# Window attention ahead of two gated networks: the mask as four 64x64 fp32 products, and the end of attention written out

## Chip, cores and metric

The kernel runs on one core of a Trainium2 chip. The metric is the device time of one execution in microseconds. Of the engines, PE is TensorE (PEld its weight loads), DVE is VectorE, ACT is ScalarE, POOL is GpSimd, and SP issues the DMAs.

## What is computed

```python
scores = scale * np.matmul(q, k.transpose(0, 1, 3, 2))     # 4 batches, 8 heads, 576 positions, 64 wide
rel = pos[:, None] - pos[None, :]
mask = (rel >= 0) & (rel < 64)
scores = np.where(mask, scores, -1000000000.0)
attn = np.exp(scores - np.max(scores, axis=-1, keepdims=True))
attn = attn / (np.sum(attn, axis=-1, keepdims=True) + 1e-09)
x = np.matmul(attn, v)                                      # then 2304 tokens x 512
g = x @ w_gate; x = (g / (1 + np.exp(-g)) * (x @ w_val)) @ w_out        # 512 -> 1536 -> 512
out = ((x @ w1) * (x @ w2) @ w3) @ w_out2                   # 512 -> 1024 -> 1024 -> 512
```

The weights of the two networks come as 64-bit floats, and are narrowed on the chip.

## The kernel before, in words

Attention comes first. A unit is a pair of heads of one batch, 16 units in all. A query block of 64 positions needs the keys of its own block and of the one before it, 128 in all; three such blocks of a pair make a subtile of 128 rows (64 of each head) by 3 x 128 scores, in one PSUM bank. A step m of the loop takes two subtiles, 2m and 2m + 1; there are NM = 24 steps. The work of a step is spread over four of them, so that engines overlap: `emit_S` (the mask and the scores) and `emit_max` in step m, `emit_exp` of its two subtiles at the end of step m and in step m + 1, `emit_norm` in m + 1 (reciprocal of the sums on VectorE, the products on GpSimd), `emit_PT` (transposes of the probabilities) in m + 2, `evac_PT` (their copies from PSUM to the tile ptt, on VectorE) and `emit_PV` (the products with v) in m + 3, whose result `evac_PV` copies to the tiles X on ScalarE. `emit_T` transposes q and k for coming units, two or three parts a step, and `evac_T` copies them. Each engine runs its instructions in the order in which this loop emits them.

The mask is added by TensorE: for each subtile, one product of a scaled 128x128 identity `identr` with a tile of 128 x 384 mask values opens the accumulation, both of the type that TensorE reads as rounded fp32 (F32R). The scores are then 64x64 products of q with 128 key columns, of plain fp32; `place` puts the two heads of a subtile in quarters of the array such that four products, of two subtiles and two heads, use four different quarters. A product of plain fp32 shows as two records in the trace, one of F32R as one.

Between these instructions a planner (`Plan`) sets work for the first network. It keeps a clock `now`, and for each engine the time until which it is taken (`free`, raised by `charge`); `advance(us)` moves the clock on and emits queued jobs of engines that are free before it. Jobs are the narrowing and splitting of weights (w_g, w_v; st_g and st_v are what is loaded), and the operands of the first network (xo): X is cut in quarter blocks, sums of blocks are formed, and each is cast to F32R on ScalarE (`cast`, L200) with the remainder formed on VectorE (`rest`, L204; sums are L208). An operand is ready once both are done. `slots` counts tiles of 128 x 768 words that are free for jobs; ATTENTION = 26 of 56 are kept for attention until its end.

The first network multiplies by a scheme of seven products in place of eight (numbered 1, 2, 5, 6, 7, 4, 3 in order); each is six F32R instructions of 384 columns. Its products are emitted by the generator `gate`, one for each `next`. In the last three rounds of the loop (m = 24, 25, 26), where there is no S, `during_attention` takes 3, 2 and 2 products from `gate`. xo is made for three blocks of 768 tokens; names such as xo0_51 stand for block 0, product 5, second half.

Of the kernel before, what the change touches and what calls it, by code (L numbers as in the profile page):

```python
# [7 lines left out]
F32 = mybir.dt.float32  # L8
F32R = mybir.dt.float32r
I32 = mybir.dt.int32  # L10
I64 = mybir.dt.int64
AF = mybir.ActivationFunctionType
# [4 lines left out]
P = 128  # L17
# [15 lines left out]
def window_attention_moe_kernel(ctx: ExitStack, tc: tile.TileContext, q, k, v, w_gate, w_val, w_out, w1, w2, w3, w_out2, out):  # L33
    nc = tc.nc
# [5 lines left out]
    KC = DM // P  # L40
# [20 lines left out]
    def slot(shape, dtype, name, counted=True):  # L61

        plan.slots -= counted
        return sl.tile(shape, dtype, tag="s", name=name)
# [266 lines left out]
            X[tp, c] = slot([P, TP], F32, f"X{tp}_{c}")  # L331
        return X[tp, c]

    def attention(events, filling):
        if True:
            ident, identr = own.tile([P, P], F32, name="ident"), own.tile([P, P], F32R, name="identr")
            masktiles = [slot([P, 2, SUB, P], F32R, f"mask{x}", False) for x in range(2)]
            mask = [masktiles[0][:, 0], masktiles[0][:, 1], masktiles[1][:, 0]]

            units = [(b, pr) for b in range(B) for pr in range(PAIRS)]  # L340
# [39 lines left out]
            def evac_T(u, part):  # L380
                which, x = divmod(part, 2)
                o = tbank.pop((u, part)).rearrange("p g n -> p (g n)")
                to = kT if which else qT
                if x == 0:
                    to[u] = slot([P, S], F32, f"{'qk'[which]}T{u}", False)
                dst = to[u][:, S // 2 * x:S // 2 * x + S // 2]
                if which == 0:
                    nc.scalar.mul(out=dst, in_=o, mul=0.125)
                elif x == 1:
                    nc.scalar.copy(out=dst, in_=o)  # L390
                else:
                    nc.vector.tensor_copy(out=dst, in_=o)
# [6 lines left out]
            def emit_S(m):  # L399
                both = (2 * m, 2 * m + 1)  # L400
                for i in both:
                    sc[i] = bank(f"S{i}")[:, :SUB * P].rearrange("p (j k) -> p j k", j=SUB)
                    nc.tensor.matmul(sc[i], lhsT=identr, rhs=mask[i % NSUB], start=True, stop=False)
                for jj in range(SUB):
                    for i in both:
                        u, s = divmod(i, NSUB)
                        j = SUB * s + jj
                        keys = kT[u].rearrange("p (w n) -> p w n", n=64)

                        keys = keys[:, :2] if j == 0 else keys[:, j - 1:j + 1] if j % 2 else keys[:, j - 1:j + 1][:, ::-1]  # L410
                        for h in range(2):
                            r, c = 64 * h, 64 * place(i, h)
                            nc.tensor.matmul(sc[i][c:c + 64, jj, :], lhsT=qT[u][r:r + 64, 64 * j:64 * j + 64],  # L413
                                             rhs=keys[r:r + 64], start=False,
                                             stop=jj == SUB - 1)

            def emit_max(m):
                st = own.tile([P, 4, 2, SUB], F32, tag="stat", name=f"stat{m}", bufs=3)
                for x in range(2):
                    nc.vector.tensor_reduce(out=st[:, 0, x, :], in_=sc[2 * m + x], op=ALU.max, axis=AX.X, negate=True)  # L420
                stat[m] = st
# [91 lines left out]
            for x in ((0, 0), (0, 1), (0, 2), (0, 3), (1, 0)):  # L513
                emit_T(*x)
                evac_T(*x)
            for m in range(NM + 3):

                u0, r = 2 * (m // 3), m % 3
                for u in ((u0 + 3,), (), (u0 + 4,))[r]:
                    if u < U:  # L520
                        load_qk(u)
                for u in ((u0 + 1,), (u0 + 2,), ())[r]:
                    if u < U:
                        load_v(u)
                parts = (((u0 + 1, 1), (u0 + 1, 2), (u0 + 1, 3)), ((u0 + 2, 0), (u0 + 2, 1)),
                         ((u0 + 2, 2), (u0 + 2, 3), (u0 + 3, 0)))[r]
                parts = [x for x in parts if x[0] < U]
                if m < NM:
                    emit_S(m)
                if m >= 3:  # L530
                    evac_PT(m - 3)
                for x in parts:
                    emit_T(*x)
                if m >= 3:
                    emit_PV(m - 3)
                if 2 <= m < NM + 2:
                    emit_PT(m - 2)
                if 1 <= m <= NM:
                    emit_exp(2 * m - 1)
                if m == NM:  # L540

                    nc.scalar.activation(out=masks[:, 0, :1], in_=masks[:, 1, :1], func=AF.Silu)
                if m < NM:
                    emit_max(m)
                for x in parts:
                    evac_T(*x)

                filling(m, NM)
                if 1 <= m <= NM:
                    emit_norm(m - 1)  # L550
                for u in ((), (u0,), (u0 + 1,))[r]:
                    if u < U:
                        pair_v(u)
                if m >= 3:
                    evac_PV(m - 3)
                if m < NM:
                    emit_exp(2 * m)
                events(m, NM)


    PRODUCT = 1.04
# [591 lines left out]

    gate = gated(xop1, left1, order1, AF.Silu, h1d, events1)

    def during_attention(m, NM):
        if m in (1, 3):
            loads(1 + m // 2)
        if m == 3:
            make_to(left1[0, 1], 0)  # L1160
        for tp, first in enumerate((13, 20, NM + 2)):
            if m == first:
                xop1[tp] = Operands([X[tp, c] for c in range(KC)], f"xo{tp}")
        if m < NM:
            plan.fill(("DVE",))
        else:
            for e, cost in (("DVE", (1.6, 1.1, 1.1)), ("ACT", (2.2, 0.5, 0.5)), ("POOL", (1.9, 0.0, 0.0))):
                plan.charge(e, cost[m - NM])
            for _ in range((3, 2, 2)[m - NM]):
                next(gate)  # L1170

    def filling(m, NM):
        if m < NM:
            for e, cost in (("DVE", 2.75), ("ACT", 3.2), ("POOL", 2.6)):
                plan.charge(e, cost)
            plan.advance(3.85, ("ACT", "POOL", "SP"))

    with tc.manual_schedule():
        plan.shut.add("POOL")
        attention(during_attention, filling)  # L1180
        plan.slots += ATTENTION
        plan.ahead = 1.0
        for _ in gate:
            pass
        for _ in project(rows, wos, events_p):
            pass
        on(events2, len(order2) - 6, lambda: make_to(w3s[-1]))
        begin_e, run_e = final(rows2)

        def put_all():  # L1190
            for j in by:
                plan.need(j)
            begin_e()
        on(events2, len(order2) - 4, put_all)
        for _ in gated(xop2, left2, order2, AF.Copy, h2d, events2):
            pass
        run_e()
# [30 lines left out]
```

## Time and profile before

| | |
|---|---|
| median of 3 runs | 848.73 us (847.08 to 850.55) |
| profiled execution | 848.98 us |
| its span, first to last instruction | 847.3 us |
| PE, PEld, DVE, ACT, POOL busy | 97%, 93%, 76%, 53%, 7% of the span |
| mean granted clock of TensorE | 0.996 of full |
| HBM | 160 GB/s over the span |

Busy shares are means over stages with different limits. A line number is that of the kernel before; in the changed kernel lines stand lower (L403 becomes L406, L413 L417, L452 L456, L583 L600). In a timeline, neighbouring instructions of one kind are merged, and what stands in brackets is the idle time of the engine ahead of the row and what ended it.

### The profile page before, as it was taken

The numbers are of one execution on the slowest core, as the hardware profiler recorded it, in microseconds if no ns is written. First come the engines' busy times: TensorE is split into PE (matmuls) and PEld (weight loads), VectorE is DVE, ScalarE is ACT, GpSimd is POOL, SyncE is SP. The second block draws the span as 40 slices with busy tenths as digits, with TensorE's granted clock in tenths as the row PEclk, the third lists the DMA queues.
The fourth block names the chain that finished last, engine by engine and source line by source line (L and its number), as shares of the span: only waits on it lengthen the run. The fifth ranks groups of instructions, "written<-read, shape, count | busy, mean of one in ns | idle before, by whom it ended". The sixth has DMA issues, their size and how long they took to land.

```text
span 847.3 us, 15757 instructions
## 1 busy us (share of the span) xinstructions
PE 822.9 (97%) x5870; PEld 791.6 (93%) x5870; DVE 642.5 (76%) x1364; ACT 451.2 (53%) x1188; POOL 60.8 (7%) x89
## 2 busy tenths in 40 slices
PE   7899878899999999999999999999999999999998
PEld 6688767899999999999999999999999998899998
DVE  4799779878688767976698585778788844788884
ACT  6799855564646464643563362544444423766452
POOL 3467600000000000000000000000000000000000
PEclk9999999999999999999999999999999999999999
DMA  9989200135255324689996851015555329623522
GB/s 203 219 174 211 72 1 38 46 121 189 97 207 191 142 91 162 224 301 385 374 307 183 227 200 50 1 75 161 149 167 170 121 83 353 214 78 124 173 75 75
DMA packets 147516, 136.29 MB, mean 161 GB/s; under 512 B 95088, under 2 KB 114288, under 8 KB 146416
## 3 DMA queue, kind: packets, MB, share of 16 engines
q1 hardware_dynamic: 147440, 135.29, 51.0%
q8 instruction: 46, 0.75, 0.4%
q14 instruction: 30, 0.25, 0.1%
HBM read 92.27 MB, written 42.99 MB: 160 GB/s over the span
## 4 chain that ended last, share of the span: by engine, by line
PE 80%; DMA 7%; DVE 4%; SPq 4%; ACT 4%; issue 1%; ACTq 0%; DVEq 0%
PE ala L583 14%; PE alb L583 13%; PE o L723 12%; PE beb L583 7%; PE bea L583 7%; PE al L947 6%; PE acc L881 5%; PE gaa L583 3%; PE gab L583 3%; PE be L947 3%; DMA wo<-wo 2%; SPq L350 2%; PE PV L466 2%; PE ga L947 2%; ACT pexp L427 1%; PE PT L446 1%
## 5 line engine op out<-in xcount | busy, mean ns | idle before, releaser
L723 PE MATMUL o<-ph,wo 128*128 128x384 f32 x576 | 146.7, 334 | 0.2 <-DVE X L710 0.2
L723 PEld LDWEIGHTS o<-ph,wo 128*128 128x128 f32 x576 | 104.2, 188 | 0.5 <-DVE X L710 0.5
L723 PE MATMUL o<-pl,wo 128*128 128x384 f32 x288 | 96.3, 334 | 0.1
L590 ACT COPY ha<-ala 128x384 f32<-128x384 f32 x90 | 42.7, 478 | 57.6 <-PE ala L583 51.2
L594 DVE TENSOR_TENSOR ha<-ha,bea 128x384 f32<-128x384 f32 x60 | 33.2, 553 | 35.8 <-PE bea L583 19.9
L723 PEld LDWEIGHTS o<-pl,wo 128*128 128x128 f32 x288 | 54.1, 188 | 0.4 <-DVE pl L204 0.4
L427 ACT ACTIVATE pexp<-S,stat 128x128 f32<-128x128 f32 x144 | 53.8, 432 | 0.0
L604 ACT ACTIVATE ha<-ha 128x384 f32<-128x384 f32 x54 | 28.3, 526 | 39.1 <-DVE ha L594 39.1
L204 DVE TENSOR_TENSOR hf<-h,hf 128x384 fp32r<-128x384 f32 x84 | 43.5, 553 | 5.6 <-ACT hf L200 5.6
L200 ACT CAST ph<-pl 128x768 fp32r<-128x768 f32 x36 | 29.2, 836 | 34.4 <-DMA pl<-h 27.7
L200 ACT CAST hf<-h 128x384 fp32r<-128x384 f32 x84 | 39.3, 513 | 13.0 <-DVE h L208 11.4
L204 DVE TENSOR_TENSOR pl<-pl,ph 128x768 fp32r<-128x768 f32 x36 | 33.5, 952 | 13.0 <-ACT ph L200 12.5
L437 POOL TENSOR_TENSOR pexp<-pexp,stat 128x384 f32<-128x384 f32 x48 | 38.7, 826 | 41.7 <-DVE stat L434 37.2
L590 ACT COPY c12b<-alb 128x384 f32<-128x384 f32 x30 | 14.4, 480 | 49.4 <-PE alb L583 49.3
L427 ACT ACTIVATION_READ_ACCUMULATOR pexp<-S,stat 128x1 f32 x144 | 38.3, 270 | 0.0
L594 DVE TENSOR_TENSOR c22b<-c22b,beb 128x384 f32<-128x384 f32 x30 | 16.6, 555 | 27.1 <-ACT c22b L590 27.0
L583 PE MATMUL ala<-xo,w_g_6l 128*128 128x384 f32 x90 | 29.6, 338 | 1.6 <-ACT xo L200 1.0
L420 DVE TENSOR_REDUCE stat<-S 128x3 f32<-128x384 f32 x48 | 24.4, 551 | 7.4 <-PE S L413 7.2
L583 PE MATMUL ala<-xo,w_g_1h 128*128 128x384 f32 x120 | 27.7, 345 | 1.7 <-ACT w_g_1h L200 1.7
L466 PE MATMUL PV<-ptt,v 128*64 128x64 f32 x576 | 22.8, 229 | 5.1 <-DVE ptt L452 2.3
L917 ACT COPY o<-al 128x256 f32<-128x256 f32 x36 | 13.4, 373 | 27.0 <-PE al L947 26.0
L466 PEld LDWEIGHTS PV<-ptt,v 128*64 128x64 f32 x576 | 19.5, 139 | 8.8 <-issue 3.8
(533 smaller groups left out, 2490.2 us busy)
## 6 DMA issues: line engine op xcount, KB each, us to landing
h<-ha SPq DMA_DIRECT2D x60, 384.0 KB, 3.2
pl<-h SPq DMA_DIRECT2D x36, 384.0 KB, 6.4
h<-h SPq DMA_DIRECT2D x24, 384.0 KB, 4.9
st_w<-in_moe_w_dram SPq DMA_DIRECT2D x8, 1024.0 KB, 6.3
st_g<-in_moe_w_gate_dram SPq DMA_DIRECT2D x6, 1024.0 KB, 6.3
st_v<-in_moe_w_val_dram SPq DMA_DIRECT2D x6, 1024.0 KB, 5.5
st_wo<-in_moe_w_out_dram SPq DMA_DIRECT2D x6, 1024.0 KB, 5.4
wo<-by_wo SPq DMA_DIRECT2D x12, 512.0 KB, 3.7
```

Of the source, the lines that this page charges most:

```text
L200: (eng.copy if eng is nc.scalar else eng.tensor_copy)(out=hi(), in_=src())
L204: return plan.job(lambda eng: eng.tensor_tensor(out=lo(), in0=src(), in1=hi().bitcast(F32), op=ALU.subtract), after, slots=slots, DVE=dve( ...
L427: nc.scalar.activation(out=pe[:, jj, :], in_=so[:, jj, :], func=AF.Exp, bias=st[:, 0, x, jj:jj + 1], accum_out=st[:, 1, x, jj:jj + 1])
L437: nc.gpsimd.tensor_tensor(out=pe, in0=pe, in1=st[:, 3, x, :].unsqueeze(2).to_broadcast([P, SUB, P]), op=ALU.mult)
L466: nc.tensor.matmul(pp[64 * h:64 * h + 64, 64 * (SUB * x + jj):64 * (SUB * x + jj) + 64], lhsT=vt[u][e][:, at, h, :], rhs=t[:, x, jj, c:c + ...
L583: nc.tensor.matmul(acc, lhsT=self.wt.ops[p, x][:, m, :], rhs=self.xs.ops[p, m][:, y, :], start=start and n == 0, stop=n == 5, skip_group_c ...
L590: nc.scalar.copy(out=out, in_=src)
L594: nc.vector.tensor_tensor(out=out, in0=x, in1=y, op=ALU.add)
L604: nc.scalar.activation(out=h, in_=src, func=func)
L723: nc.tensor.matmul(acc[m, x], lhsT=wos.tiles[i // 6][:, i % 6, :], rhs=rows[2 * tp + x].words(f, b), start=f == n == 0, stop=f == NF - 1 a ...
L881: nc.tensor.matmul(acc, lhsT=w3T[i][c // 3][:, x, (c % 3) * P:(c % 3) * P + P], rhs=zt[c, y], start=c == k == 0, stop=c == NI - 1 and k == 2)
L947: nc.tensor.matmul(acc, lhsT=self.xs.ops[p, m][:, x, t * P:t * P + P], rhs=right.ops[p, m, y], start=start and n == 0, stop=n == 3 * R - 1 ...
```

## The change

`identr` and the mask tiles become plain fp32. In `emit_S` the two 128x128 products are replaced by four of 64x64, with the rows r of the identity and of the mask and the output rows c that the scores of the same head use.

The loop ends at m = 23, and what was in its last three rounds stands behind it, line by line, with calls of `drain` between: each gives tiles back, charges the engines, and takes a product from `gate` (0, 1, 3), moves the clock (2) or queues the operands of block 2 (4). In step 23 the copies of step 21's transposes stand right behind the maximum, and the planner's filling comes behind the exponentials. The v copies of two units come a step earlier at the end.

`during_attention` gives back some of the 26 kept tiles in steps 18 to 23 (HELD) instead of all at the end. In a step the planner's clock moves by 3.55 instead of 3.85 (3.1 in step 23), with the same charges.

```diff
-            ident, identr = own.tile([P, P], F32, name="ident"), own.tile([P, P], F32R, name="identr")
-            masktiles = [slot([P, 2, SUB, P], F32R, f"mask{x}", False) for x in range(2)]
+            ident, identr = own.tile([P, P], F32, name="ident"), own.tile([P, P], F32, name="identr")
+            masktiles = [slot([P, 2, SUB, P], F32, f"mask{x}", False) for x in range(2)]
...
-                    nc.tensor.matmul(sc[i], lhsT=identr, rhs=mask[i % NSUB], start=True, stop=False)
+                for i in both:
+                    for h in range(2):
+                        r, c = 64 * h, 64 * place(i, h)
+                        nc.tensor.matmul(sc[i][c:c + 64], lhsT=identr[r:r + 64, r:r + 64], rhs=mask[i % NSUB][r:r + 64],
+                                         start=True, stop=False)
...
-            for m in range(NM + 3):
+            for m in range(NM):
...
+                if m == NM - 1:
+
+                    evac_PT(m - 2)
+                else:
+
+                    filling(m)
...
+            emit_PV(NM - 3)
+            emit_exp(2 * NM - 1)
+            emit_norm(NM - 1)
+            evac_PV(NM - 3)
+            nc.scalar.activation(out=masks[:, 0, :1], in_=masks[:, 1, :1], func=AF.Silu)
+            drain(0)
+            for x in range(2):
+                emit_PT(NM - 2 + x)
+                evac_PT(NM - 2 + x)
+                drain(1 + 2 * x)
+                emit_PV(NM - 2 + x)
+                evac_PV(NM - 2 + x)
+                drain(2 + 2 * x)
...
+    HELD = {18: 24, 19: 22, 20: 18, 21: 16, 22: 12, 23: 7}
+    HELD_END = (4, 4, 4, 2, 0)
+    held = [ATTENTION]
+    def hold(n):
+        plan.slots += held[0] - n
+        held[0] = n
+    def operands(tp):
+        xop1[tp] = Operands([X[tp, c] for c in range(KC)], f"xo{tp}")
+    def during_attention(m):
+        if m in HELD:
+            hold(HELD[m])
+        if m in (13, 20):
+            operands(m // 20)
+        plan.fill(("DVE",) if m not in HELD or m < 23 else ("DVE", "ACT"))
+    def filling(m):
+        for e, cost in (("DVE", 2.75), ("ACT", 3.2), ("POOL", 2.6)):
+            plan.charge(e, cost)
+        if m == 23:
+            plan.advance(3.1, ("DVE", "ACT", "POOL", "SP"))
-            plan.advance(3.85, ("ACT", "POOL", "SP"))
+            plan.advance(3.55, ("ACT", "POOL", "SP"))
+    def drain(n):
+        hold(HELD_END[n])
+        for e, cost in (("DVE", (0.4, 1.1, 0.0, 1.1, 0.0)), ("ACT", (3.0, 0.0, 0.6, 0.0, 0.6))):
+            plan.charge(e, cost[n])
+        if n == 4:
+            operands(2)
+        else:
+            next(gate) if n in (0, 1, 3) else plan.advance(0.8)
```

What it moves shows in the order of instructions at three places.

TensorE at the scores of step 20, before and now (S40 and S41 are its subtiles, PT35 transposes of an earlier one, T14 a transpose of keys to come; x2 is two neighbouring instructions):

```order
L446 MATMUL PT35_1778<-ident_128,pexp35_1704 128x128 x3
L403 MATMUL S40_1810<-mask0_130,identr_129 128x384
L403 MATMUL S41_1812<-mask1_131,identr_129 128x384
L413 MATMUL S40_1810<-kT13_1712,qT13_1622 64x128 x2
L413 MATMUL S41_1812<-kT13_1712,qT13_1622 64x128 x2
...
L376 MATMUL T14_2_1829<-ident_128,rawk14_1557 128x96 x3
```

```order
L450 MATMUL PT35_1789<-ident_128,pexp35_1718 128x128 x3
L406 MATMUL S40_1818<-mask0_130,identr_129 64x384 x2
L406 MATMUL S41_1819<-mask1_131,identr_129 64x384 x2
L417 MATMUL S40_1818<-kT13_1726,qT13_1634 64x128 x2
L417 MATMUL S41_1819<-kT13_1726,qT13_1634 64x128 x2
...
L376 MATMUL T14_2_1839<-ident_128,rawk14_1567 128x96 x3
```

Each subtile has two mask products of 64 rows in place of one of 128, two per bank and four in all ahead of the scores; nothing else moves.

VectorE from the maximum of step 23, before (first fence) and now (second):

```order
L420 TENSOR_REDUCE stat23_2084<-S46_2040 128x3
L420 TENSOR_REDUCE stat23_2084<-S47_2042 128x3
L204 TENSOR_TENSOR xo0_51_2038<-X0_1_528,xo0_51_2038 128x384
L208 TENSOR_TENSOR X0_0_447<-X0_2_698,X0_0_447 128x384
L433 TENSOR_SCALAR stat22_2020<-stat22_2020 128x6
L434 RECIPROCAL stat22_2020<-stat22_2020 128x6
L452 COPY ptt21_2103<-PT42_2072 128x384
L452 COPY ptt21_2103<-PT43_2076 128x384
L433 TENSOR_SCALAR stat23_2084<-stat23_2084 128x6
L434 RECIPROCAL stat23_2084<-stat23_2084 128x6
L594 TENSOR_TENSOR ha0_0_0_2137<-ha0_0_0_2137,gaa0_0_2147 128x384
L208 TENSOR_TENSOR X0_1_528<-X0_3_776,X0_1_528 128x384
```

```order
L424 TENSOR_REDUCE stat23_2095<-S46_2049 128x3
...
L456 COPY ptt21_2098<-PT42_2083 128x384
...
L437 TENSOR_SCALAR stat22_2030<-stat22_2030 128x6
...
L437 TENSOR_SCALAR stat23_2095<-stat23_2095 128x6
...
L204 TENSOR_TENSOR xo0_10_2136<-X0_0_455,xo0_10_2136 128x384
L204 TENSOR_TENSOR xo0_11_2139<-X0_1_537,xo0_11_2139 128x384
L204 TENSOR_TENSOR w_v0_2l_2149<-st_v0_461,w_v0_1h_1982 128x256
L208 TENSOR_TENSOR st_v0_461<-st_v0_461 128x2x128
L208 TENSOR_TENSOR X0_0_455<-X0_0_455 128x384
L456 COPY ptt22_2163<-PT44_2155 128x384
...
L204 TENSOR_TENSOR xo0_20_2167<-X0_2_709,xo0_20_2167 128x384
L204 TENSOR_TENSOR xo0_21_2170<-X0_3_789,xo0_21_2170 128x384
```

The copies to ptt21 come ahead of both reciprocals. Behind them stand operands of products 1 and 2 of block 0 and a part of w_val, which before were made in steps 13 to 22; up to the last maximum 27 planned operations stand on VectorE where there were 42 (on ScalarE 13 and 26).

TensorE behind the last scores, before and now (PV products with v, ala, gaa, bea products 1/6/7, 2 and 5 of the first unit, alb product 1 of the next):

```order
L446 MATMUL PT43_2076<-ident_128,pexp43_2016 128x128 x3
L466 MATMUL PV21_2106<-ptt21_2103,v14_0_1730 64x64 x4
...
L446 MATMUL PT45_2123<-ident_128,pexp45_2080 128x128 x3
L583 MATMUL ala0_0_2139<-xo0_10_1297,w_g0_1h_782 128x384 x3
...
L583 MATMUL gaa0_0_2147<-xo0_20_1470,w_g0_1h_782 128x384 x2
...
L583 MATMUL bea0_0_2156<-xo0_50_1974,w_g0_2l_943 128x384 x2
...
L466 MATMUL PV22_2168<-ptt22_2165,v14_1_2029 64x64 x2
...
L446 MATMUL PT47_2185<-ident_128,pexp47_2127 128x128 x3
L583 MATMUL ala0_0_2139<-xo0_60_2191,w_g0_5l_1022 128x384 x2
...
L583 MATMUL alb0_0_2206<-xo0_10_1297,w_v0_1h_1215 128x384 x3
...
L466 MATMUL PV23_2220<-ptt23_2217,v15_0_1896 64x64 x2
...
L583 MATMUL ala0_0_2139<-xo0_70_2234,w_g0_6l_1110 128x384 x2
```

```order
L450 MATMUL PT43_2087<-ident_128,pexp43_2026 128x128 x3
L470 MATMUL PV21_2110<-ptt21_2098,v14_0_1739 64x64 x4
...
L600 MATMUL ala0_0_2135<-xo0_10_2136,w_g0_1h_969 128x384 x3
...
L450 MATMUL PT45_2159<-ident_128,pexp45_2091 128x128 x3
L600 MATMUL gaa0_0_2166<-xo0_20_2167,w_g0_1h_969 128x384 x2
...
L470 MATMUL PV22_2187<-ptt22_2163,v14_1_1974 64x64 x2
...
L450 MATMUL PT47_2208<-ident_128,pexp47_2123 128x128 x3
L600 MATMUL bea0_0_2215<-xo0_50_2216,w_g0_2l_1123 128x384 x3
...
L470 MATMUL PV23_2237<-ptt23_2212,v15_0_1899 64x64 x2
...
L600 MATMUL ala0_0_2135<-xo0_60_2235,w_g0_6h_1306 128x384 x3
...
L600 MATMUL alb0_0_2274<-xo0_10_2136,w_v0_1h_1982 128x384 x3
...
L600 MATMUL ala0_0_2135<-xo0_70_2272,w_g0_6h_1306 128x384 x2
```

PV21 is followed by product 1, then PT44 and PT45, product 2, PV22, PT46 and PT47, product 5 and PV23; before, PT44 and PT45 came first, then products 1, 2 and 5, and two more products stood ahead of PV23.

## Rows read from the trace of the kernel before

**Rows 1.** Windows by stage: PE, PEld, DVE, ACT, POOL busy, PEclk, DMA share, GB/s.

```profile
50.00:65.00 15.00, 15.00 (x271) 12.43 (x269) 14.86 (x39) 14.95 (x73) 9.89 (x15) 1.00 0.81 176
...
95.00:105.00 10.00, 7.82 (x97) 7.02 (x96) 5.60 (x15) 7.41 (x30) 7.37 (x10) 0.83 0.01 2
105.00:115.00 10.00, 6.91 (x75) 5.55 (x73) 6.26 (x13) 3.74 (x10) 0.00 (x0) 1.00 0.00 0
```

**Rows 2.** Timeline of PE in a middle step: start, length, instructions, idle before.

```profile
51.19 0.59 PE L403 MATMUL S<-mask,identr 128*128 128x384 f32 x2
51.71 0.89 PE L413 MATMUL S<-kT,qT 64*64 64x128 f32 x24
52.52 0.72 PE L376 MATMUL T<-ident,rawk 96*128 96x96 f32 x6
...
54.27 0.87 PE L446 MATMUL PT<-ident,pexp 128*128 128x128 f32 x6
54.89 0.59 PE L403 MATMUL S<-mask,identr 128*128 128x384 f32 x2
```

**Rows 3.** Timeline of PE in attention's last steps and behind it.

```profile
91.50 0.60 PE L403 MATMUL S<-mask,identr 128*128 128x384 f32 x2
...
94.59 0.60 PE L403 MATMUL S<-mask,identr 128*128 128x384 f32 x2
...
99.98 1.21 PE L466 MATMUL PV<-ptt,v 128*64 128x64 f32 x24 [2.08 <-issue]
...
102.32 2.06 PE L583 MATMUL ala<-xo,w_g_1h 128*128 128x384 f32 x6
...
107.63 0.94 PE L466 MATMUL PV<-ptt,v 128*64 128x64 f32 x24 [1.17 <-DVE ptt L452]
...
116.62 0.51 PE L583 MATMUL gab<-xo,w_v_1h 128*128 128x384 f32 x2
...
117.66 1.20 PE L583 MATMUL beb<-xo,w_v_5h 128*128 128x384 f32 x6
```

**Rows 4.** Instructions of line L413: engine, operation, nanoseconds of one.

```profile
L413 PE MATMUL S<-kT,qT x576: 269/269/473, 8.5 to 95.7; 64*64 64x128 f32 x192
```

**Rows 5.** Timeline of PE in the first ten steps.

```profile
24.28 0.69 PE L376 MATMUL T<-ident,rawq 96*128 96x96 f32 x6 [2.02 <-DMA rawq<-in_q_dram]
...
27.10 1.05 PE L403 MATMUL S<-mask,identr 128*128 128x384 f32 x2
...
34.45 1.03 PE L466 MATMUL PV<-ptt,v 128*64 128x64 f32 x24 [0.50 <-DVE ptt L452]
...
38.75 0.94 PE L466 MATMUL PV<-ptt,v 128*64 128x64 f32 x24 [0.58 <-ACT pexp L427]
...
44.02 0.59 PE L403 MATMUL S<-mask,identr 128*128 128x384 f32 x2
```

**Rows 6.** DMA queues from 15 to 45 us: packets, MB, share of 16 engines.

```profile
q1 hardware_dynamic: 18222, 6.35, 100.1%
```

**Rows 7.** Waits, 0 to 46 us: total us, times, longest.

```profile
DVE st_v L188 <- DMA st_v<-in_moe_w_val_dram: 1.8, 1, 1.8
```

**Rows 8.** Timeline of DVE behind the last step.

```profile
106.00 1.02 DVE L208 TENSOR_TENSOR X<-X,X 128x384 f32<-128x384 f32 x2
```

**Rows 9.** Timeline of ACT behind the last step.

```profile
97.46 0.37 ACT L427 ACTIVATE pexp<-S,stat 128x128 f32<-128x128 f32 x1
...
98.49 0.52 ACT L200 CAST xo<-X 128x384 fp32r<-128x384 f32 x1
...
100.09 1.28 ACT L542 ACT_TABLE_LOAD   x1
...
109.04 0.94 ACT L200 CAST xo<-X 128x384 fp32r<-128x384 f32 x2
```

**Rows 10.** Waits, 117 to 170 us.

```profile
PE bea L583 <- DVE xo L204: 2.7, 2, 1.7
...
PE ala L583 <- ACT xo L200: 1.6, 2, 1.1
```

More of the change, by code (lines that the diff above doesn't have):

```diff
@@ L332, in x_tile, with attention @@
         return X[tp, c]
-    def attention(events, filling):
+    def attention(events, filling, drain):
         if True:
-            ident, identr = own.tile([P, P], F32, name="ident"), own.tile([P, P], F32R, name="identr")
-            masktiles = [slot([P, 2, SUB, P], F32R, f"mask{x}", False) for x in range(2)]
+            ident, identr = own.tile([P, P], F32, name="ident"), own.tile([P, P], F32, name="identr")
+            masktiles = [slot([P, 2, SUB, P], F32, f"mask{x}", False) for x in range(2)]
             mask = [masktiles[0][:, 0], masktiles[0][:, 1], masktiles[1][:, 0]]
@@ L527, in attention @@
                 parts = [x for x in parts if x[0] < U]
-                if m < NM:
-                    emit_S(m)
+                emit_S(m)
                 if m >= 3:
@@ L535, in attention @@
                     emit_PV(m - 3)
-                if 2 <= m < NM + 2:
+                if m >= 2:
                     emit_PT(m - 2)
-                if 1 <= m <= NM:
+                if m >= 1:
                     emit_exp(2 * m - 1)
[L540 to L544, printed above, removed]
+                emit_max(m)
                 for x in parts:
                     evac_T(*x)
-                filling(m, NM)
-                if 1 <= m <= NM:
+                if m == NM - 1:
+                    evac_PT(m - 2)
+                else:
+                    filling(m)
+                if m >= 1:
                     emit_norm(m - 1)
-                for u in ((), (u0,), (u0 + 1,))[r]:
-                    if u < U:
-                        pair_v(u)
+                for u in (((), (u0,), (u0 + 1,)) if u0 + 2 < U else ((u0,), (u0 + 1,), ()))[r]:
+                    pair_v(u)
                 if m >= 3:
                     evac_PV(m - 3)
-                if m < NM:
-                    emit_exp(2 * m)
-                events(m, NM)
+                emit_exp(2 * m)
+                if m == NM - 1:
+                    filling(m)
+                events(m)
+            emit_PV(NM - 3)
[11 more added lines that the diff above has]
+                drain(2 + 2 * x)
     PRODUCT = 1.04
@@ L1154, in window_attention_moe_kernel @@
     gate = gated(xop1, left1, order1, AF.Silu, h1d, events1)
-    def during_attention(m, NM):
+    HELD = {18: 24, 19: 22, 20: 18, 21: 16, 22: 12, 23: 7}
[9 more added lines that the diff above has]
+            hold(HELD[m])
         if m in (1, 3):
@@ L1160, in during_attention @@
             make_to(left1[0, 1], 0)
[L1161 to L1165, printed above, removed]
-        else:
[L1167 to L1175, printed above, removed]
-            plan.advance(3.85, ("ACT", "POOL", "SP"))
+        if m in (13, 20):
[6 more added lines that the diff above has]
+            plan.advance(3.1, ("DVE", "ACT", "POOL", "SP"))
+        else:
+            plan.advance(3.55, ("ACT", "POOL", "SP"))
[7 more added lines that the diff above has]
+            next(gate) if n in (0, 1, 3) else plan.advance(0.8)
     with tc.manual_schedule():
         plan.shut.add("POOL")
-        attention(during_attention, filling)
-        plan.slots += ATTENTION
+        attention(during_attention, filling, drain)
         plan.ahead = 1.0
```

## Prediction

> **What bounds the kernel now.** I read the stretches first, then TensorE's timeline in one step, then the end of attention, then the waits behind it. In the middle of attention TensorE is busy all of a 15 us stretch, and VectorE and ScalarE nearly so [rows 1]; which of the three sets the pace is told by the timeline: no TensorE instruction there has idle time ahead of it, and one step follows the other after 3.70 us [rows 2]. So TensorE bounds the steps from 9 on; from the mask of step 9 to that of step 22 the pitch is (91.50 - 44.02) / 13 = 3.65 us [rows 3, 5]. VectorE and ScalarE are full because the planner fills them with work for later. The first steps are bound by transfers: the DMA engines are full [rows 6], TensorE waits 2.02 us for q and then runs a while at 1.2 instead of 2.4 GHz (the mask pair takes 1.05 against 0.59) [rows 2, 5]. Behind the last mask (94.59) TensorE works in pieces: 2.08 us idle, product 1 in 2.06 us where six such instructions later take 1.20, another 1.17 us idle for ptt [rows 3]; the granted clock is 0.83 of full from 95 to 105, and VectorE is busy for only 6.26 of the 10 us behind [rows 1]. The first units of the network also wait, for operands [rows 10]. The rest of the run is TensorE at work and the same in both kernels.
>
> **The change part by part.**
>
> *Mask.* In the rows, S is three sets of four 64x64 products with 128 columns each, two records per product. Its 24 records take 0.89 us, of which 0.27 is the length of the last [rows 2, 4]; 0.62 for the five gaps between six sets is 0.12 each, or 0.11 without the weight load that only the first waits for. So a set of four runs at once, and 128 columns cost 0.11 per record, 0.22 per product. The new mask is one set of four with 384 columns, as many columns as all of S: 6 x 0.11 = 0.65 us. The old pair takes 0.52 from its start to that of S (51.19 to 51.71) [rows 2]; six 384-column products of its kind elsewhere give (1.20 - 0.33) / 5 = 0.174 each [rows 3], so 0.35 of it is streaming and 0.17 is the turn from 128 rows to 64. That turn now stands ahead of the mask instead of behind it. Cost: 0.65 - 0.35 = +0.30 us per step. Bounds: +0.13 if no turn is left ahead of the mask (0.65 against 0.52), +0.39 with 0.12 per record (0.74 against 0.35). I take 0.30, since the turn between S and T is also paid [rows 2]. Fourteen steps from 9 to 22 lie wholly on TensorE: 14 x 0.30 = **+4.2 us** at the last mask.
>
> The Trainium skill, "TensorE: Matmul & The Clock Gate", section "Back-to-back issue gap", gives N/2.4 + 2.5 ns per matmul, 56 ns at 128 columns; the rows above show twice that per record, as the 4 passes of true fp32 in "FP8 and Floating Point Precision", section "TensorE Precision Notes", would make it. By the first page alone, with two records, the new mask would cost 0.33 us and the steps would stay as they are, some 849.5 in all; the rows decide for the second.
>
> *First nine steps.* There the 0.30 a step is paid while TensorE would wait anyway. Its 2.02 us wait for q ends when the transfer lands, not earlier or later; four masks, one at the low clock, use up about 1.5 of it, and a wait of 0.5 should not lower the clock as this one did. That spares some 0.5 of the mask pair and as much again in the instructions about it. Two further waits, 0.50 and 0.58 [rows 5], come from VectorE, which stood 1.8 us on a weight transfer in step 6 [rows 7]; in the changed order that instruction comes a step later, behind the landing. Transfers still set the earliest start of steps 5 to 8. Spared 2.0 + 1.0 + 1.1 = 4.1, paid 9 x 0.30 plus 0.3 for the cold first mask = 3.0, and about 0.6 of new waiting for k and q: **-0.5 us** (bounds -1.5 and +2.0).
>
> *Less work between the steps.* The planner now moves on by 3.55 per step instead of 3.85. The order shows what that does: up to the last maximum VectorE gets 27 planned operations instead of 42, ScalarE 13 instead of 26. Given-back tiles do not help: in steps 18 to 22 there are six such operations on VectorE where before there were eleven. While TensorE bounds a step of 3.95 us, that lightening gains nothing. The price is at the end: of block 0's operands nothing is ready, where six casts and rests (xo_10, 11, 20, 21, 30, 50) were, and w_val is split as far as its first product.
>
> *The end*, counted from the last mask. Durations: VectorE on 384 columns 0.47 apiece (two in 1.02) [rows 8]; three exponentials 1.03, a cast 0.41, the table load 1.28 [rows 9]; a product 1.04 (116.62 to 117.66), PV 0.85, PT 0.65 [rows 2, 3]. S ends at 1.6, the maxima at 2.6, ptt of PT 42/43 at 4.2, so PV 21 starts at 4.2, where it started at 5.4: a gain of 1.2. Then product 1 needs xo_10 and xo_11, which ScalarE casts behind exponentials (to 4.7), an eviction and table load (6.9): casts 7.3 and 7.7, rests to 8.2, product 1 ends 8.7, PT 44/45 at 9.5. VectorE has a weight rest, a sum and X_0 to do (9.5), then ptt, xo_20 and xo_21: 11.5; product 2 ends 11.9, PV 22 12.8, PT 46/47 13.5. Then an addition, four weight rests, the last two behind ScalarE's casts (14.1), ptt, xo_50, X_1, a cast and xo_51 to 17.0: product 5 ends 17.4, PV 23 18.3. Two sums and xo_60 follow, and xo_61, cast behind PV's eviction, ends 19.7; product 6 ends 20.1, product 1 of the next unit 21.1; with seven more VectorE operations product 7 ends 23.5. Before it ended at 116.62 - 94.59 = 22.0. So **+1.5 us**, bounds -8.4 (no wait left, second rival) and +6 (third). VectorE's idle time here is what pays most of the late work.
>
> *Behind it.* Two rests of block 0 are still owed (+0.95), two of block 1 are done earlier, and the waits for operands [rows 10] are shortened by as much: **-0.5**, bounds -3 and +1.
>
> Sum: 848.98 (the profiled execution: span 847.3 and 1.7 around it; 0.25 above the median of three) + 4.2 - 0.5 + 1.5 - 0.5 = **853.7 us**.
>
> **The rivals.**
> *The mask costs no more than the pair.* If its two records ran 384 columns as fast as the old kind does, 2 x 0.174 stand against 0.35. For it, sets of four have only been seen with short columns, where four weight loads could be what takes 0.11; against it, the length of one record, 0.269 at 128 columns, against 0.33 for 384 columns of the other type [rows 3, 4], for a third of the columns 0.8 of the length. Then 848.98 - 0.5 + 1.5 - 0.5 = 849.5.
> *Faster: the end wins.* If the operand work keeps ahead of TensorE, nothing waits between the last mask and product 7: S 1.6, four PV, three PT and six products with their turns between make 13.6 where 22.0 stood, -8.4, and part of rows 10 goes too, about -2. Time 848.98 + 3.7 - 10.4 = 842.3. It decides at product 5: xo_51 must be there by about 13.5 on that clock, not 17.0. VectorE's 6.26 of 10 busy [rows 1] speaks for it; the order, with eleven operations between ptt 22 and xo_51, against.
> *The clock falls.* TensorE idles 2.3 us before product 1, as long as where it fell before [rows 3, 5], and again about product 5; five products, PT and PV at half rate add up to 5: 859.
> *The change does not do what it says*: the tiles given back change nothing visible; that is already in the forecast.
>
> **How the numbers follow.** Forecast 0.58, mask for nothing 0.20, end wins 0.12, clock falls 0.10. A measurement here tells 0.5% (4.2 us) from no change: below 844.5 is faster, above 853.0 slower. The forecast's own range, from the bounds of its terms, is 849.5 to 858 and lies above 853.0 in two thirds of cases (0.39); with the last case 0.49 slower. Faster is most of the second rival and a little of the first, 0.14; the rest, 0.37, is the same. The range leaves out the best of the second rival and the worst of the last: 846 to 860.
>
> **What would show it.** Mask records in sets of four, second set 0.33 behind the first, S 0.65 behind the mask; pitch of the middle steps 3.95 with no TensorE idle; VectorE with some 0.6 us idle a step; q's wait near 24 us shortened below 1 us; product 7 done some 23.5 us behind the last mask, with TensorE waiting for xo before products 1, 2 and 5. Wrong if the pitch stays at 3.65 or falls, or if product 5 finds xo_51 ready.

## The result and the profile after

The changed kernel takes **859.98 us** (median of 4 runs, 859.26 to 861.41) where the kernel before, on the same chip, takes 849.13 (847.08 to 850.55): ratio 1.0117, 95% interval 1.0087 to 1.0148. It is slower, by 10.85 us and not by the 4.7 forecast. The profiled spans are 857.8 and 847.3 us, 10.5 apart, so the traces hold nearly all of it.

The windows by stage of the changed kernel, against [rows 1] (busy time of PE, PEld, DVE, ACT and POOL, then the granted clock):

```profile
50.00:65.00 15.00, 15.00 (x271) 11.67 (x266) 11.49 (x33) 13.55 (x65) 9.18 (x13) 1.00 0.83 185
95.00:105.00 10.00, 6.83 (x149) 5.31 (x140) 6.23 (x18) 9.64 (x42) 8.20 (x12) 1.00 0.01 2
105.00:115.00 10.00, 8.60 (x49) 6.39 (x49) 7.43 (x17) 4.26 (x12) 0.18 (x1) 0.66 0.00 0
```

TensorE is still busy all of a middle stretch, but VectorE for 11.49 of 15 us where it was 14.86. From 105 to 115 TensorE has 0.66 of its clock, where it had all of it.

TensorE's timeline in a middle step, against [rows 2], and the mask's line in the view by line (busy us, mean ns of one record):

```profile
46.59 0.87 PE L450 MATMUL PT<-ident,pexp 128*128 128x128 f32 x6
47.40 0.88 PE L406 MATMUL S<-mask,identr 64*64 64x384 f32 x8
48.09 0.83 PE L417 MATMUL S<-kT,qT 64*64 64x128 f32 x24
48.86 0.71 PE L376 MATMUL T<-ident,rawq 96*128 96x96 f32 x6
...
51.16 0.88 PE L406 MATMUL S<-mask,identr 64*64 64x384 f32 x8
...
L406 PE MATMUL S<-mask,identr 64*64 64x384 f32 x192 | 22.4, 523 | 0.0
```

The mask is eight records, two per product. It starts 0.81 behind PT (54.89 - 54.27 = 0.62 before), S starts 0.69 behind the mask (0.52 before), T 0.77 behind S (0.81 before): some 0.3 us more a step, and no idle time.

TensorE at attention's end, against [rows 3]:

```profile
97.60 0.88 PE L406 MATMUL S<-mask,identr 64*64 64x384 f32 x8
...
101.15 0.99 PE L470 MATMUL PV<-ptt,v 128*64 128x64 f32 x24 [0.37 <-issue]
104.95 0.44 PE L600 MATMUL ala<-xo,w_g_1h 128*128 128x384 f32 x1 [2.81 <-ACT xo L200]
...
106.98 1.48 PE L450 MATMUL PT<-ident,pexp 128*128 128x128 f32 x6
...
111.47 1.55 PE L470 MATMUL PV<-ptt,v 128*64 128x64 f32 x24
...
115.25 0.62 PE L600 MATMUL bea<-xo,w_g_2l 128*128 128x384 f32 x2 [0.58 <-DVE xo L204]
116.26 1.60 PE L600 MATMUL bea<-xo,w_g_2l 128*128 128x384 f32 x3 [0.40 <-ACT xo L200]
...
119.27 2.27 PE L600 MATMUL ala<-xo,w_g_6h 128*128 128x384 f32 x6
...
125.19 0.51 PE L600 MATMUL gab<-xo,w_v_1h 128*128 128x384 f32 x2
```

The last mask comes at 97.60 (94.59 before: +3.0). Product 7 ends where gab begins, 27.6 us behind it (22.0 before: +5.6). The rest of the span is 10.5 - 8.6 = 1.9 us longer. TensorE waits for operands before products 1, 2, 5 and 7; behind the waits of 2.81 and of 0.58 and 0.40 us, PT, PV and product 6 take 1.7 to 1.9 times their time (1.48, 1.55 and 2.27 us for 0.87, 0.92 and 1.20).

### The profile page after: what moved, and what is told of

It reads as the page before. It is cut to its first block, busy times and chain, and to the rows that moved or that the text cites. A ratio compares the mean times of both kernels' runs of the same rounds, so it can differ in the third digit from the quotient of the medians.

```text
span 857.8 us, 16042 instructions
## 1 busy us (share of the span) xinstructions
PE 832.9 (97%) x6014; PEld 793.3 (92%) x6014; DVE 640.1 (75%) x1364; ACT 453.8 (53%) x1188; POOL 58.7 (7%) x89
## 4 chain that ended last, share of the span: by engine, by line
PE 83%; DMA 6%; DVE 4%; SPq 4%; ACT 2%; issue 1%; DVEq 0%; ACTq 0%
PE ala L600 14%; PE o L740 13%; PE alb L600 13%; PE bea L600 7%; PE beb L600 7%; PE al L964 6%; PE acc L898 5%; PE gaa L600 3%; PE gab L600 3%; PE be L964 3%; SPq L350 2%; PE PV L470 2%; DMA zd<-by_z 2%; PE PT L450 2%; PE ga L964 2%; PE S L406 2%
## 5 line engine op out<-in xcount | busy, mean ns | idle before, releaser
L431 ACT ACTIVATE pexp<-S,stat 128x128 f32<-128x128 f32 x144 | 51.7, 393 | 0.0
L204 DVE TENSOR_TENSOR hf<-h,hf 128x384 fp32r<-128x384 f32 x84 | 43.5, 552 | 5.7 <-ACT hf L200 5.6
L441 POOL TENSOR_TENSOR pexp<-pexp,stat 128x384 f32<-128x384 f32 x48 | 38.7, 827 | 44.8 <-DVE stat L438 27.9
L431 ACT ACTIVATION_READ_ACCUMULATOR pexp<-S,stat 128x1 f32 x144 | 33.4, 232 | 0.0
L600 PE MATMUL ala<-xo,w_g_1h 128*128 128x384 f32 x120 | 27.6, 342 | 5.1 <-ACT xo L200 2.8
L600 PE MATMUL alb<-xo,w_v_7h 128*128 128x384 f32 x114 | 27.5, 334 | 0.0
L456 DVE COPY ptt<-PT 128x384 f32<-128x384 f32 x48 | 24.1, 542 | 4.4 <-PE PT L450 4.1
L600 PEld LDWEIGHTS ala<-xo,w_g_1h 128*128 128x128 f32 x120 | 21.4, 189 | 6.0 <-ACT xo L200 2.9
```

Source lines behind the costliest of these rows:

```text
L204: return plan.job(lambda eng: eng.tensor_tensor(out=lo(), in0=src(), in1=hi().bitcast(F32), op=ALU.subtract), after, slots=slots, DVE=dve( ...
L431: nc.scalar.activation(out=pe[:, jj, :], in_=so[:, jj, :], func=AF.Exp, bias=st[:, 0, x, jj:jj + 1], accum_out=st[:, 1, x, jj:jj + 1])
L441: nc.gpsimd.tensor_tensor(out=pe, in0=pe, in1=st[:, 3, x, :].unsqueeze(2).to_broadcast([P, SUB, P]), op=ALU.mult)
L600: nc.tensor.matmul(acc, lhsT=self.wt.ops[p, x][:, m, :], rhs=self.xs.ops[p, m][:, y, :], start=start and n == 0, stop=n == 5, skip_group_c ...
```

## The experiments

All are compared with the kernel before on the same chip; "us" is the median. That kernel took 850.02 us beside e1 to e4, 850.79 beside e5 to e8 and 849.54 beside e9 to e12, so a difference between two of these groups, or between one of them and the change, is uncertain by a microsecond or two. "End" is the time from the last mask to the end of product 7, and "VectorE" its busy time from 45 to 90 us (of 45), both from the profiled execution.

| kernel | us | ratio, 95% interval | end | VectorE |
|---|---|---|---|---|
| before | 849 to 851 | 1 | 22.0 | 44.2 |
| the change | 859.98 | 1.0117 (1.0087 to 1.0148) | 27.6 | 35.0 |
| e1_mask | 854.38 | 1.0045 (1.0027 to 1.0064) | 21.8 | 39.4 |
| e2_old_mask | 855.80 | 1.0062 (1.0047 to 1.0077) | 27.9 | 38.4 |
| e3_advance | 855.22 | 1.0054 (1.0034 to 1.0073) | 19.3 | 39.4 |
| e4_end | 850.54 | 1.0004 (0.9989 to 1.0018) | 19.5 | 44.2 |
| e5_steps | 859.12 | 1.0089 (1.0065 to 1.0112) | 30.2 | 38.4 |
| e6_busy | 858.07 | 1.0072 (1.0046 to 1.0098) | 25.2 | 34.8 |
| e7_split | 846.49 | 0.9940 (0.9920 to 0.9960) | 18.5 | 43.5 |
| e8_longer | 848.34 | 0.9971 (0.9956 to 0.9986) | 15.7 | 43.9 |
| e9_no_tiles | 862.78 | 1.0158 (1.0128 to 1.0188) | 28.7 | 35.0 |
| e10_long_no_tiles | 851.94 | 1.0027 (1.0006 to 1.0049) | 16.5 | 43.8 |
| e11_long_split | 846.51 | 0.9964 (0.9945 to 0.9983) | 16.9 | 42.2 |
| e12_split_more | 850.18 | 1.0006 (0.9990 to 1.0022) | 20.0 | 44.1 |

### The change taken apart: e1 to e5

**e1_mask**, the kernel before with the new mask:

```diff
...
-                    nc.tensor.matmul(sc[i], lhsT=identr, rhs=mask[i % NSUB], start=True, stop=False)
...
+                        nc.tensor.matmul(sc[i][c:c + 64], lhsT=identr[r:r + 64, r:r + 64], rhs=mask[i % NSUB][r:r + 64],
+                                         start=True, stop=False)
```

> The kernel before with the four 64x64 fp32 products for the mask and nothing else (3.85 a step for the planner, the old end). Theory: the mask lies on TensorE from step 9 on, 14 x 0.29 = 4.1 us, less some 0.5 that the first nine steps hide, so the last mask comes some 3.5 us later, the end keeps its 22 us, and the run takes 852.6 us (851.5 to 853.8). Rival: the longer step gives VectorE and ScalarE 0.29 us more for planned work in each step, the end gets shorter by as much as an operand or two, and the run takes 850.5 or less.

Measured +0.45% or 3.8 us, as the theory has it, though 854.38 lies 0.6 us above its range, where the kernel before took 850.02; the rival is out.

**e2_old_mask**, the change with those lines the other way round.

> The changed kernel with the old mask (one product of the quick type per half step) in place of the new. Theory: the mask's cost comes off and nothing else moves, since the order of the other work is fixed by the planner: pitch back to 3.65, last mask some 3.6 us earlier, product 7 still some 27 us behind it, 856.3 us (855 to 857.5), so that 7 us of the loss are the end's and not the mask's. Rival: with less time per step VectorE and ScalarE fall behind in the steps, and only 1 to 2 us come off, 858 to 859.

Measured 855.80: 4.2 us off, the end as long as before the edit. So about 5 us are not the mask's.

**e3_advance**, the change with

```diff
-            plan.advance(3.55, ("ACT", "POOL", "SP"))
+            plan.advance(3.85, ("ACT", "POOL", "SP"))
```

> The changed kernel with the planner moving on by 3.85 a step instead of 3.55, and nothing else: 12 more planned VectorE rows (36 instead of 24) stand ahead of the last maximum, among them the rests of xo_10 to xo_50. Theory (late operands): the end's loss came from operand work pushed behind the last maximum; with it done in the steps, product 7 ends 18 to 20 us behind the last mask instead of 27.6, TensorE keeps 2.4 GHz through it, and the run takes 849 us (846 to 851). Rival (the written-out end itself, ptt and PV between the products): product 7 still 25 us or more behind the last mask, 857 to 860. Second rival (VectorE cannot do the twelve in the steps): pitch above 4.1 us, 855 or more.

**e4_end**, the same with the old mask as well.

> The changed kernel with the old mask and with 3.85 a step: what is left of the change is the end written out and the tiles given back from step 18. Theory (late operands): this is the better half of the change, product 7 ends 18 to 20 us behind the last mask where the kernel before has 22.0, and the run takes 845 us (842.5 to 847.5), faster than both kernels. Rival (the written-out end itself): 853 to 857. Rival (the end gains nothing, since what it saves is waited for in the next units): 848 to 850.

In both the end shrinks as the first theory says, to 19.3 and 19.5 us, and the time only to 855.22 and 850.54, against 849 and 845 expected. e4 shows where it goes. Product 7 ends 3.0 us earlier than before (113.63 against 116.62), and the lead is still 2.85 behind the next wait for an operand (126.35 against 129.20 at the product that follows it). But behind that wait e4's TensorE works at half rate, and that of the kernel before does not (timelines, first before, then e4_end):

```profile
127.47 0.44 PE L583 MATMUL bea<-xo,w_g_2l 128*128 128x384 f32 x1 [1.67 <-DVE xo L204]
...
130.79 1.23 PE L583 MATMUL alb<-xo,w_v_4h 128*128 128x384 f32 x6
131.86 1.20 PE L583 MATMUL beb<-xo,w_v_3h 128*128 128x384 f32 x6
132.90 1.20 PE L583 MATMUL alb<-xo,w_v_1h 128*128 128x384 f32 x6
```

```profile
124.62 0.45 PE L596 MATMUL bea<-xo,w_g_2l 128*128 128x384 f32 x1 [2.30 <-DVE xo L204]
...
129.20 2.12 PE L596 MATMUL alb<-xo,w_v_4h 128*128 128x384 f32 x6
131.12 1.61 PE L596 MATMUL beb<-xo,w_v_3h 128*128 128x384 f32 x6
132.57 1.20 PE L596 MATMUL alb<-xo,w_v_1h 128*128 128x384 f32 x6
```

The windows from 120 to 130 us show the clock, 1.00 before and 0.76 in e4_end, at much the same busy time:

```profile
120.00:130.00 10.00, 7.04 (x38) 6.15 (x37) 8.41 (x18) 7.28 (x18) 0.00 (x0) 1.00 0.00 1
```

```profile
120.00:130.00 10.00, 7.13 (x28) 5.90 (x27) 8.46 (x18) 5.66 (x14) 0.00 (x0) 0.76 0.00 0
```

From 127.43 to 132.57 e4 waits for no operand and takes 5.14 us for what took 3.09 before; 0.3 us of the lead is left. Later waits, some shorter and some longer, take that too, and the profiled span ends at the same 847.3 us. So the written-out end by itself is worth nothing at 3.85, as the last rival of e4 has it but for half a us, but most of what it wins is lost to the clock behind a wait rather than to a longer wait. No run kept the clock up there, so what the lead would then be worth is open. Whether VectorE's and ScalarE's work for operands decides is what the later runs take up.

e3 also lost time in the first steps. VectorE stands in step 6 on w_val's transfer, and PV stands behind the ptt copy that is queued behind that (timelines of DVE and PE, e3_advance):

```profile
34.23 0.43 DVE L188 TENSOR_SCALAR st_v<-st_v 128x512 int32<-128x512 int32 x1 [4.29 <-DMA st_v<-in_moe_w_val_dram]
...
35.45 1.55 PE L470 MATMUL PV<-ptt,v 128*64 128x64 f32 x24 [2.53 <-DVE ptt L456]
```

This is the wait of [rows 7], longer and with TensorE at half rate behind it. At 3.55 it is gone, as the instruction comes a step later.

**e5_steps**, the kernel before with 3.55.

> The kernel before with the planner moving on by 3.55 a step instead of 3.85, and nothing else: old mask, old end. Theory (VectorE's time in the steps is thrown away): VectorE then idles in each step from 9 on, and what it leaves undone is work that the first units of the network wait for, whichever way the end is written. The first nine steps win about 1 us, the rest pays, 854.9 us (853 to 857), as much as the step from the old mask at 3.85 with the new end (850.5) to the same at 3.55 (855.8). Rival (the deferral only hurts the new end, whose order has ptt ahead of the operands): 849 to 851.

Measured 859.12, 8 us lost and not 5. The rival fell: the old end suffers from the deferral too. Up to product 7 it suffers as much as the new one, 7.1 us in the traces (123.74 against 116.62) and 7.2 from e4 to e2 (120.86 against 113.63). What the old end loses beyond that (e2, the same but for the end and the tiles, takes 855.80) comes in the units behind: the whole spans are 9.5 and 7.3 us longer. This was not taken further. So the pieces add up only in part: mask 3.8 to 4.7 us (before to e1, e2 to the change, e4 to e3; the last pair is no clean price, since in the traces e3 is 4.1 us behind e4 before step 9, by the wait shown above), deferral 4.8 (e3 to the change) and 5.3 (e4 to e2) with the new end, 8 with the old.

### The clock: e6

**e6_busy** keeps TensorE at work in two of the gaps:

```diff
+            po = bank("still")
+            for n in range(24):
+                nc.tensor.transpose(po[:, P * (n % 4):P * (n % 4) + P], ident, ident)
             evac_PV(NM - 3)
...
+                if x:
+                    po = bank("still")
+                    for n in range(12):
+                        nc.tensor.transpose(po[:, P * (n % 4):P * (n % 4) + P], ident, ident)
                 drain(1 + 2 * x)
```

> The changed kernel with TensorE kept at work where it idles at attention's end: 24 transposes of the identity into a bank that nobody reads behind PV 21 (ahead of product 1), and 12 more ahead of product 5. The output is the same. Theory (the clock costs there): the granted clock stays at 2.4 GHz, PT 22, product 2, PV 22, PV 23 and product 6 take their usual times instead of 1.5 to 2.3 us, product 7 ends some 23.5 us behind the last mask, and the run takes 856 us (854.5 to 857.5). Rival (operands set the time, half rate or not): the lengths shrink and the waits for xo grow by as much, product 7 ends within 1 us of 27.6 behind the last mask, 858.5 to 861.

The windows from the last mask to product 7, first the change, then e6_busy:

```profile
97.60:125.20 27.60, 21.28 (x184) 15.41 (x184) 18.42 (x44) 16.65 (x54) 5.96 (x8) 0.81 0.10 31
```

```profile
98.12:123.30 25.18, 20.99 (x219) 16.14 (x219) 18.39 (x44) 16.66 (x54) 5.96 (x8) 1.00 0.11 33
```

The same work of VectorE and ScalarE to 0.03 us, the clock at 2.4 GHz throughout, and the end 2.4 us shorter. That is 2.4 of the 4.1 us that the first theory expected at product 7: at full rate TensorE waits longer for xo before product 2, 0.96 us for 0.34, and the waits of 0.57 and 0.40 within product 5 stay. The whole span is 855.1, 2.7 shorter, but near 180 us the lead is 1.0 (product starts at 184.39 against 185.40), so the rest of it arises far from the edit. The medians are 1.9 apart, on two chips and with overlapping intervals; the clock's price is read from the traces.

### VectorE's time in the steps: e7, e8, e11, e12

**e7_split**, with the old mask; **e8_longer**, with the new one:

```diff
-            plan.advance(3.55, ("ACT", "POOL", "SP"))
+            plan.advance(3.55 if m < 9 else 3.85, ("ACT", "POOL", "SP"))
```

```diff
-            plan.advance(3.55, ("ACT", "POOL", "SP"))
+            plan.advance(4.15, ("ACT", "POOL", "SP"))
```

> The changed kernel with the old mask, and the planner moving on by 3.55 a step up to step 8 and by 3.85 from step 9: no wait on the weight transfer in the first steps, VectorE full behind them. Theory: the last mask comes at about 93, 1 to 2 us earlier than with 3.85 all through, and half of it is left at the end, 849 us (847 to 850.3), a little below both kernels. Rival (all of it is given back to the operands of the next units, since VectorE's work decides): 850 to 851.5.

> The changed kernel, new mask and new end, with the planner moving on by 4.15 a step: 46 planned VectorE rows ahead of the last maximum where the changed kernel has 24 and the kernel before 36. Theory (VectorE's work up to the fifth unit or so decides): a step that TensorE makes 0.29 us longer is no loss if VectorE uses it, the waits for xo behind the end shrink by what was done early, and the run takes 851.5 us (849.5 to 853). Rival (the mask's 4.2 us adds whatever VectorE does): 854 to 856, as with 3.85. Second rival (VectorE and ScalarE cannot do it in a step of 3.95): pitch above 4.05 us, 856 or more.

Both beat the kernel before, and both came in below the range that their theories gave (847 to 850.3, and 849.5 to 853). e8 is the change with one number altered, and 11.6 us faster than it. Its pitch is the change's 3.93 (step 9 at 46.62, step 22 at 97.72), and the mask costs what it did; but VectorE uses the longer step. ScalarE does too: the planner's time holds for both, and no run gave it back to one of them alone, so how the loss divides between the two engines is open. The view by windows from 45 to 90 us, of the kernel before, the change, and e8_longer:

```profile
45.00:90.00 45.00, 45.00 (x793) 37.33 (x785) 44.24 (x112) 44.95 (x212) 30.86 (x42) 1.00 0.88 181
```

```profile
45.00:90.00 45.00, 45.00 (x805) 35.35 (x805) 35.00 (x91) 40.58 (x186) 27.71 (x39) 1.00 0.83 181
```

```profile
45.00:90.00 45.00, 45.00 (x804) 35.19 (x807) 43.89 (x109) 44.20 (x202) 27.94 (x38) 1.00 0.90 197
```

And the end of e8_longer on TensorE, where products 1, 2, 5 and 6 wait for no operand, only PV for ptt:

```profile
101.17 0.88 PE L406 MATMUL S<-mask,identr 64*64 64x384 f32 x8
...
105.44 1.03 PE L470 MATMUL PV<-ptt,v 128*64 128x64 f32 x24 [0.26 <-DVE ptt L456]
106.40 1.34 PE L600 MATMUL ala<-xo,w_g_1h 128*128 128x384 f32 x6
...
110.08 0.94 PE L470 MATMUL PV<-ptt,v 128*64 128x64 f32 x24 [0.47 <-DVE ptt L456]
...
113.66 1.33 PE L600 MATMUL ala<-xo,w_g_7l 128*128 128x384 f32 x6
...
116.91 0.51 PE L600 MATMUL gab<-xo,w_v_1h 128*128 128x384 f32 x2
```

**e11_long_split** is e8 with 3.55 before step 7, **e12_split_more** e7 with 3.95 for 3.85.

> The changed kernel, new mask and new end, with the planner moving on by 3.55 a step up to step 6 and by 4.15 from step 7. Theory (both walls): VectorE no longer stands on the weight transfer in step 6 (with 4.15 all through that cost some 3.5 us at step 7), and is full behind it; 41 planned rows ahead of the last maximum against 46 give half of it back, 846.3 us (844.5 to 848). Rival (what is won early is lost in full, five rows at 0.5 us and their casts): 848 to 849.5.

> The old mask and the new end, with 3.55 a step up to step 8 and 3.95 from step 9, where the run with 3.85 took 846.5 us. Theory (VectorE and ScalarE are full at 3.85 with a step of 3.65 on TensorE): nothing is gained, 846.5 us (845 to 848.5), and more idle time shows on TensorE in the last steps. Rival (there is still room): 843 to 845.

e11 came in as expected, with the wait on w_val gone; it and e7 are the fastest, 3.0 and 4.3 us below their kernel before. e12 missed both expectations. More planned work did not fit: in the last steps TensorE idles 0.70 us ahead of a PV, until a cast on ScalarE ends, and 0.96 for ptt (its timeline), and behind product 6 it works at half rate again:

```profile
92.52 0.94 PE L466 MATMUL PV<-ptt,v 128*64 128x64 f32 x24 [0.70 <-ACT xo L200]
...
96.46 0.94 PE L466 MATMUL PV<-ptt,v 128*64 128x64 f32 x24 [0.96 <-DVE ptt L452]
```

How the 3.7 us by which it is slower than e7 divide between these was not taken further.

### The tiles: e9, e10

```diff
-    HELD = {18: 24, 19: 22, 20: 18, 21: 16, 22: 12, 23: 7}
-    HELD_END = (4, 4, 4, 2, 0)
+    HELD = {}
+    HELD_END = (26, 26, 26, 26, 0)
...
-        plan.fill(("DVE",) if m not in HELD or m < 23 else ("DVE", "ACT"))
+        plan.fill(("DVE",) if m < 23 else ("DVE", "ACT"))
```

in the change (**e9_no_tiles**) and in e8 (**e10_long_no_tiles**).

> The changed kernel without the tiles given back from step 18: all 26 reserved tiles come free at the end of attention, as before; mask, end and 3.55 a step as changed. Theory (nothing in the steps waits for a tile at 3.55): VectorE's rows stand in the same order up to the rest of xo_60, and the run takes 859.5 us (858 to 861). Rival (the tiles carry the operand work at the end): 862 or more.

> As the changed kernel with 4.15 a step (848.3 us), but without the tiles given back from step 18: 42 planned VectorE rows stand ahead of the last maximum instead of 46. Theory (the tiles are worth what VectorE can do early with them): four rows of about 0.5 us move behind the last maximum, 850.3 us (849 to 852). Rival (the tiles are worth nothing there either): 847.5 to 848.9.

e9 is 2.8 us slower than the change, so its rival came true and not its theory; e10 is 3.6 slower than e8, within its theory's range. The intervals of e9 and the change overlap (1.0128 to 1.0188 and 1.0087 to 1.0148), those of e10 and e8 do not: the tiles help, by an amount that is not settled. In e9 the steps are the same to 0.07 us at the last mask. It loses 1.1 us by product 7, at product 6, whose operand is cast later, so that TensorE idles and then works at half rate (its timeline):

```profile
119.84 2.56 PE L600 MATMUL ala<-xo,w_g_6h 128*128 128x384 f32 x6 [0.99 <-ACT xo L200]
122.20 2.12 PE L600 MATMUL alb<-xo,w_v_1h 128*128 128x384 f32 x6
```

Some more goes further on: from 140 to 150 us its granted clock is 0.70, that of the change 0.98.

## Why the prediction was right in direction and short in size

The measured 859.98 lies above the forecast's own range, 849.5 to 858, and inside 846 to 860 by 0.02 us; the upper end of that came from the third rival, which gave 859 and had 0.10. That the wider range holds the result is luck as far as the forecast goes.

**Mask, +4.2: right.** 0.30 us a step, and 3.6 us from the mask of step 9 to the last (14 pitches: 97.60 - 43.39 against 94.59 - 44.02; two of the old pitches held 0.2 to 0.3 us more, of which the change shows nothing). In the whole time 3.8 to 4.7. The first rival is out: from mask to S are 0.69 us, near the 0.65 worked out from [rows 2, 4], and not two times 0.174. The Trainium skill, "TensorE: Matmul & The Clock Gate", section "Back-to-back issue gap", gives by its formula for the gap of one product an estimate of 384/2.4 + 2.5 = 163 ns a record, 0.33 us for the two; the trace shows twice that, and agrees with the four passes of true fp32 that the Trainium skill names in "FP8 and Floating Point Precision", section "TensorE Precision Notes".

**First nine steps, -0.5: right.** The mask of step 9 comes at 43.39, 0.63 earlier; in e9 and e6, which are the same up to there, it comes at 43.46 and 43.91, so the gain is 0.1 to 0.6. The wait for q at 24 us is 1.52, not below 1, but the clock no longer falls behind it.

**Less work between the steps, priced only at the end: the step that failed.** VectorE idles 3.51 of 15 us, 0.92 a step and not 0.6, and ScalarE 1.45, where it had next to none. I wrote of that lightening that it "gains nothing", carried the postponed rows into the end as a list of operations, and took VectorE's idle time there for "what pays most of the late work". e8 shows what the idle time in the steps was worth: used, it makes the end 11.9 us shorter and the run 11.6 (its last mask comes 3.6 us later, with a wait on w_val in the first steps, so that product 7 ends 8.3 earlier). A step that TensorE makes longer is no loss by itself if VectorE and ScalarE are then the engines whose work is late: e11, with the new mask, is about as fast as e7, with the old (846.51 and 846.49 us). The prediction counted both the longer step and the empty VectorE, but never the one against the other.

**The end, +1.5: mis-sized, it is +5.6**, just within its bound of 6. My clock against the trace, from the last mask: product 1 ends at 8.7 forecast, 9.4 measured; product 2 at 11.9, 13.9; product 5 at 17.4, 20.2; product 6 at 20.1, 23.8; product 7 at 23.5, 27.6. Each operand came later than on the list, and twice the waiting was followed by half rate. The third rival, "the clock falls", which I held apart from the forecast at 0.10, was not separate from it: with idle times as the forecast has them, 2.3 us before product 1 (2.81 in the trace), the clock fell. By e6 it is 2.4 us of the 4.1 missing; the other 1.7 are operands, which there too end the waits.

**The given-back tiles change nothing: wrong.** They are worth some 2.8 us by e9 and 3.6 by e10, neither figure sharp. I compared rows up to the last maximum only; the tiles move casts behind it.

**Behind it, -0.5: wrong in sign, +1.9.** One more wait, of 0.79 us behind product 7, costs 1.1 of it, and the waits for block 1's operands did not shrink. What VectorE owed was more than the two rests that I set against it.

**Second rival, the end wins**: not for this change, but e8's end of 15.7 us is near its 13.6. Even so, little of it stays as time gained: in e8 the last mask comes 6.6 us later than before, and in e4 the 3.0 us that the end wins are lost behind the next wait.

## What to carry to other kernels

When one engine sets the pace and another is full of work for later, price a change in the steps on both: what the second engine no longer does there comes back where it is late. Here VectorE did 8.9 us more from 45 to 90 us in e8 than in the change, and the run was 11.6 us shorter; from e4 to e2 it did 5.8 us less, and the run was 5.3 longer. After an edit that lengthens the step, move the planner's time by as much (here to 4.15, where the kernel before has 3.85) before judging the edit. An idle gap that you forecast on TensorE can have a second price, the slower clock behind it; put it into the forecast, not beside it.

## What the runs showed that was not expected

A wait much like another can end at either clock. In the change TensorE waits 2.04 us for a rest of xo before 136.96, and 2.06 us for a cast of w_g before 168.86. Behind the first the granted clock is 0.58, behind the second 1.00 (windows):

```profile
136.90:141.00 4.10, 3.99 (x13) 3.46 (x14) 4.10 (x10) 2.42 (x7) 0.00 (x0) 0.58 0.00 0
```

```profile
168.80:172.00 3.20, 3.14 (x16) 2.66 (x17) 2.46 (x6) 1.67 (x6) 0.00 (x0) 1.00 0.00 0
```

So a gap's length alone did not tell its second price here.

Some of VectorE's operations on two tiles took twice as long beside GpSimd's: in e4_end two rests of xo take 1.89 us while GpSimd copies v, one takes 1.03 while it normalises, and two take 1.03 when it has nothing to do (timelines of DVE and POOL):

```profile
93.74 1.89 DVE L204 TENSOR_TENSOR xo<-X,xo 128x384 fp32r<-128x384 f32 x2
...
100.47 1.03 DVE L204 TENSOR_TENSOR xo<-X,xo 128x384 fp32r<-128x384 f32 x1
...
112.03 1.03 DVE L204 TENSOR_TENSOR xo<-X,xo 128x384 fp32r<-128x384 f32 x2 [0.17 <-ACT xo L200]
```

```profile
93.72 0.60 POOL L365 COPY v<-v 64x512 f32<-64x512 f32 x1
...
99.47 3.82 POOL L437 TENSOR_TENSOR pexp<-pexp,stat 128x384 f32<-128x384 f32 x4 [0.53 <-DVE stat L434]
```

The Trainium skill, "SBUF — State Buffer", section "SBUF: two separate sides", has it that such an operation, with both inputs in SBUF, and one of GpSimd that reads SBUF lock each other out of a shared pair of ports; these rows agree, but no run took GpSimd's work away. If that is the cause, a part of VectorE's busy time in the steps is waiting, and the postponed rows are shorter once attention is over.
